# Diagonal blocks of A of chunks 0 and 1 in one set of columns, one transpose for three, one scale for all input weights, and a new order: a delta-rule attention with a feed-forward layer behind it

## The chip, the cores and the metric

One core of a Trainium2 chip runs the whole program. Times are device microseconds (us) of one execution. In the profile PE is the matmul engine TensorE (PEld its weight loads), DVE is VectorE, ACT is ScalarE, POOL is GpSimd and SP is SyncE, whose queue issues all DMAs of this kernel.

## What is computed

The reference walks 768 tokens for 4 batches of 8 heads with a head dimension of 48, and then runs a feed-forward layer on the result:

```python
for t in range(S):
    kt, vt, bt = (k_n[:, :, t], v[:, :, t], beta[:, :, t, None])
    y[:, :, t] = np.einsum('bhd,bhde->bhe', q[:, :, t], state)
    v_old = np.einsum('bhde,bhd->bhe', state, kt)
    state = state + bt[:, :, :, None] * np.einsum('bhd,bhe->bhde', kt, vt - v_old)
...
h = x @ w_in                       # x: 3072 tokens x 384, w_in: 384 x 2048
sp = np.maximum(h, 0.0) + np.log1p(np.exp(-np.abs(h)))
g = h * erf(sp)
return (g @ w_out).astype(np.float32)
```

`k_n` is k over its norm. The weights arrive as 64-bit floats.

## The kernel before

**Chunks.** The tokens are cut into 12 chunks of 64. Within a chunk the recurrence is a triangular system: a Gram matrix of the keys of each head (`gram_mm`), scaled by beta and the norms into A (`gram_a`, or `gram_ac` and `gram_am`), and the inverse of the unit triangular matrix that A makes. The two heads of a pair lie on the two halves of the 128 partitions, and 16 pairs (`BP`) stand side by side. The inverse is found for 32 by 32 diagonal blocks by substitution (`solve_row`), and `merges` joins two such blocks with small matmuls (`merge_e`, `merge_z`). Then `merge_m`, `chain_u`, `chain_s` and `chain_y` carry the state from chunk to chunk and give y.

**Chunks 0 and 1** are done first and apart. A of both lies in `A01`, `[128, 2, 16, 64]`, in a part of the room of `w_out` that is not loaded yet. `block_t` turns its diagonal blocks into `gb`. The first call turns columns 32 to 63 for all partitions, which is right for the lower 32 rows of each head; the second and third turn columns 0 to 31 for the upper 32 rows of each head. 15 steps of `row16` then solve 16 by 16 blocks on VectorE, `small_t` and `back_t` turn the result back, and `small_e`, `small_z` and `merges` put the pieces together. Chunks 2 to 11 go in five pairs: A is written to DRAM, read back as blocks (`to_dram`, `to_blocks`), solved in 31 rows mostly on GpSimd, and sent back the same way (`put_blocks`, `from_blocks2`).

**Feed-forward.** Each chunk gives 256 tokens, group g. `ffn1` multiplies by 16 blocks of `w_in`, `e_sp`, `e_erf`, `e_mul`, `e_split` and `e_rest` make the gate and split it into two f16 halves, and `ffn2` multiplies by 16 blocks of `w_out`. Group 0 uses the weights as f32. From group 1 on, weights and activations are pairs of f16 numbers under a scale that is a power of two: `x_max`, `x_all` (a matmul that spreads a maximum over all partitions) and `x_scale` find it for the activations; `w_max`, `w_all` and `w_scale` for the weights; `w_hi` and `w_lo` write the two halves over the f32 block before. Before that each piece of the weights is loaded as 64-bit numbers (`w_load`) and made f32 by `w_mask`, `w_sign`, `w_bits`, while `w_mx` takes its maximum. The input weights are in two parts: "in", the first 4 blocks in two pieces, and "in2", the other 12 in eight pieces, each part with a maximum and a scale of its own.

**Order.** All calls are first put on a list. `ORDER` is a permutation of its indices, written out by hand: the calls are made in that order, and each engine, SP with its DMAs too, runs its instructions in the order in which they were made. `ENG` names, for some places, another engine than the default. `put_v` for instance multiplies v by the key norms on GpSimd (G) unless `ENG` says VectorE (V). `fill` is a matmul of zeros whose result nobody reads; there are `WF` = 233 of them, placed by `ORDER` like everything else.

Of the kernel before, what the change touches and what calls it, by code (L numbers as in the profile page):

```python
# [15 lines left out]
P = 128  # L16
# [17 lines left out]
ORDER = (0, 1, 2, 3, 4, 46, 15, 9, 12, 8, 19, 22, 24, 27, 28, 23, 29, 30, 31, 16, 32, 33, 34, 25, 20, 2232, 2233, 2234, 2235, 2236, 2237, 2238, 2239, 2240,  # L34
# [131 lines left out]
XR = 3  # L166
YR = 3
CM = (0, 1)
WF = 233
GF = 1  # L170
TK = {}

# [6 lines left out]
def delta_ffn_kernel(ctx, tc, kT, qT, ktok, vtok, btok, w_in, w_out, cst, out):  # L179
# [313 lines left out]
    def block_t(k):  # L493
        if 0 not in gb_t:
            gb_t[0] = wide("gb", 0)
# [719 lines left out]
```

## Time and profile before

| | |
|---|---|
| median of 3 runs | 618.2 us (616.4 to 619.39) |
| the profiled execution | 621.86 us, its span 620.1 us |
| TensorE busy | 577.6 us, 93% of the span, 11,125 matmuls |
| VectorE busy | 452.4 us, 73% |
| ScalarE busy | 421.1 us, 68%, of it 157.8 us in 123 table loads |
| GpSimd busy | 285.8 us, 46% |
| fills | 233, 47.7 us of the time of TensorE |
| mean granted TensorE clock | 0.965 of full speed |

The span runs from the first to the last instruction. The 1.8 us between it and the execution's time lie around the program. A busy share is a mean over stages that differ; the tables by stage below say which engine has no idle time where.

### The profile page before, as it was taken

To read this page: it belongs to the slowest core of one execution; us is meant where nothing else is said; L and a number is where in the kernel's file an instruction comes from. 1 tells how busy PE (TensorE), PEld (TensorE's weight loads), DVE (VectorE), ACT (ScalarE), POOL (GpSimd) and SP (SyncE) were. 2 spreads that over 40 slices of the span, in tenths; PEclk is the share of its full clock that TensorE was granted. 3 is DMA by queue.
4 is the path that set the end of the run, shared out by engine and by line. 5 is a ranking of instruction groups with operands and counts; after the bars stand their busy time and mean duration, and the time that the engine had idled before them with its cause. 6 is when DMAs were issued, how large, how long until landed. Compare 5 with 4: busy or idle time off the path is not lost.

```text
span 620.1 us, 25280 instructions
## 1 busy us (share of the span) xinstructions
PE 577.6 (93%) x11125; PEld 425.6 (69%) x11125; DVE 452.4 (73%) x1006; ACT 421.1 (68%) x602; POOL 285.8 (46%) x475
## 2 busy tenths in 40 slices
PE   7943698999999999999999999999999999999996
PEld 5622466677667787777777787767777787777673
DVE  5996588897998788887887976679675776354321
ACT  2326447667767687847976888477769688589862
POOL 7031124577489874668738670438853021001310
PEclk8976599999999999999999999999999999999999
DMA  9984549737913258655460618450542320101011
GB/s 273 300 243 118 131 135 218 189 90 176 178 23 97 56 139 203 156 136 135 95 132 4 183 29 205 98 84 17 140 96 64 68 61 2 27 1 27 1 26 26
DMA packets 79502, 67.89 MB, mean 109 GB/s; under 512 B 57696, under 2 KB 67040, under 8 KB 79136
## 3 DMA queue, kind: packets, MB, share of 16 engines
q1 hardware_dynamic: 79392, 66.28, 43.7%
q8 instruction: 87, 1.43, 1.0%
q14 instruction: 23, 0.19, 0.1%
HBM read 47.38 MB, written 17.83 MB: 105 GB/s over the span
## 4 chain that ended last, share of the span: by engine, by line
PE 70%; DVE 13%; issue 5%; DMA 5%; POOL 3%; ACT 2%; SPq 1%; ACTq 0%; POOLq 0%; DVEq 0%
PE ph L921 26%; PE pr L980 9%; PE pr L982 9%; PE pr L981 9%; PE pc L680 3%; PE pc L706 2%; DMA qp<-qT 2%; PE pg L407 2%; PE pc L694 2%; PE pc L710 2%; PE pm L643 1%; PE pe L611 1%; POOL tmp L525 1%; PE pz L626 1%; POOL xb L527 1%
## 5 line engine op out<-in xcount | busy, mean ns | idle before, releaser
L921 PE MATMUL ph<-xh,w_in 128*128 128x256 f16 x1056 | 188.2, 273 | 0.3 <-DVE L L955 0.3
L921 PEld LDWEIGHTS <-w_in 128*128 128x128 f16 x1584 | 151.6, 98 | 25.4 <-issue 0.5
L253 ACT ACT_TABLE_LOAD x123 | 157.8, 1283 | 2.9 <-PEq L1208 0.7
L921 PE MATMUL ph<-xl,w_in 128*128 128x256 f16 x528 | 143.9, 273 | 0.0
L980 PE MATMUL pr<-w_out,H 128*128 128x384 f16 x352 | 115.1, 327 | 0.0
L981 PE MATMUL pr<-w_out,H 128*128 128x384 f16 x352 | 114.8, 326 | 0.0
L982 PE MATMUL pr<-w_out,H 128*128 128x384 f16 x352 | 114.8, 326 | 0.0
L210 POOL TENSOR_TENSOR H<-L,H 128x512 f16<-128x512 f32 x42 | 49.9, 1199 | 127.7 <-ACT H L215 97.4
L955 DVE SCALAR_TENSOR_TENSOR L<-ph,L 128x512 f32<-128x512 f32 x88 | 59.8, 685 | 55.2 <-ACT L L948 52.0
L943 ACT ACTIVATE L<-ph,xct 128x512 f32<-128x512 f32 x88 | 58.8, 687 | 49.4 <-PE ph L921 39.6
L525 POOL TENSOR_TENSOR tmp<-gb,xb 128x175 f32<-128x175 f32 (+15 forms) x120 | 66.0, 550 | 49.5 <-DVE xb L527 23.4
L527 POOL TENSOR_TENSOR xb<-xb,tmp 128x175 f32<-128x175 f32 (+15 forms) x120 | 70.7, 589 | 9.4
L948 ACT ACTIVATE L<-L 128x512 f32<-128x512 f32 x96 | 58.5, 626 | 0.8
L210 POOL TENSOR_TENSOR z<-v,nm 64x192 f32<-64x192 f32 x60 | 32.2, 537 | 48.1 <-DMA v<-vtok 33.1
L982 PEld LDWEIGHTS <-H 128*128 128x128 f16 x352 | 34.4, 98 | 22.8
L263 PE MATMUL pr<-zero 128*128 128x384 f16 x233 | 47.7, 354 | 1.2 <-DVE zero L259 1.2
L980 PEld LDWEIGHTS <-H 128*128 128x128 f16 x352 | 34.4, 98 | 20.1
L981 PEld LDWEIGHTS <-H 128*128 128x128 f16 x352 | 34.5, 98 | 17.8
L215 ACT CAST H<-L 128x512 f16<-128x512 f32 x54 | 32.3, 613 | 13.6 <-DVE L L955 11.6
L699 DVE TENSOR_TENSOR z<-pc,z 48x192 f32<-48x192 f32 x86 | 30.4, 354 | 15.0 <-PE pc L694 10.3
L210 DVE TENSOR_TENSOR H<-L,H 128x512 f16<-128x512 f32 x46 | 38.5, 845 | 1.6 <-ACT H L215 1.2
L686 DVE TENSOR_TENSOR z<-pc,ga 64x192 f32<-64x192 f32 x94 | 33.4, 355 | 6.1 <-PE pc L680 3.9
(205 smaller groups left out, 946.4 us busy)
## 6 DMA issues: line engine op xcount, KB each, us to landing
raw_out<-w_out SPq DMA_DIRECT2D x12, 512.0 KB, 6.4
d<-pp SPq DMA_DIRECT2D x10, 512.0 KB, 4.7
d<-A SPq DMA_DIRECT2D x20, 256.0 KB, 3.2
qp<-d SPq DMA_DIRECT2D x20, 256.0 KB, 4.8
k<-ktok SPq DMA_DIRECT2D x12, 384.0 KB, 4.3
kpg<-kT SPq DMA_DIRECT2D x24, 192.0 KB, 5.3
v<-vtok SPq DMA_DIRECT2D x48, 96.0 KB, 3.0
qp<-qT SPq DMA_DIRECT2D x24, 192.0 KB, 4.2
```

What stands on the lines that cost most here:

```text
L210: {"V": ve, "G": ge}[pick(d)].tensor_tensor(*a, **kw)
L253: se.add_instruction(mybir.InstLoadActFuncSet(name=nc.get_next_instruction_name(), act_func_set_id=i, ins=[], outs=[]))
L263: te.matmul(pr[1][:, :DM], zero[:, :P], zero[:, :DM], start=new, stop=new)
L525: eng.tensor_tensor(tv, g.unsqueeze(1).broadcast_to([P, ncol, nr]), Xv[:, :, s:s + 1].broadcast_to([P, ncol, nr]), op=ALU.mult)
L527: eng.tensor_tensor(Xv[:, :, s + 1:], Xv[:, :, s + 1:], tv, op=ALU.add)
L921: te.matmul(ph, w[:, i, kt * P:kt * P + P], G[x][:, :, ksl], start=(m == 0), stop=(m == 8))
L943: se.activation(unit(g, u), G["ph", u], AF.Softplus, bias=0.0, scale=G["ct"][:, part(EU * u):part(EU * u) + 1] if g >= GF else 1.0)
L948: se.activation(Lu, Lu, AF.Erf, bias=0.0, scale=1.0)
L955: ve.scalar_tensor_tensor(Lu, fg[g]["ph", u], HSC, Lu, op0=ALU.mult, op1=ALU.mult)
L980: te.matmul(G["po"][a], gh[:, o, asl], wout_h[:, i, :], start=(i == 0), stop=False)
L981: te.matmul(G["po"][a], gh[:, o, asl], wout_l[:, i, :], start=False, stop=False)
L982: te.matmul(G["po"][a], gl[:, o, asl], wout_h[:, i, :], start=False, stop=(i == NFF - 1))
```

## The change

`gram_mm` of chunks 0 and 1 makes each 64 by 64 product of the keys in two matmuls of 32 stationary columns. The first writes the upper 32 rows with all 64 columns. The second writes the lower 32 rows with columns 32 to 63, twice side by side. So columns 0 to 31 of `A01` hold the diagonal block of every group of 32 partitions, and one `block_t` turns them all; `small_e` reads them there. "in" and "in2" become one part of ten pieces with one maximum and one scale (`NA` = 16, `RI`), and the columns of scales shrink from two to one. `WF` goes from 233 to 281. `ORDER` (2,465 entries, now 2,508) and `ENG` are replaced as a whole; the 48 added fills, less two `block_t` and the three calls `w_max`, `w_all`, `w_scale` of the second part, are the 43 more.

```diff
-RI = {"in": "EH", "in2": "EHLHLHLH"}
-NA = 4
+RI = {"in": "EHEHLHLHLH"}
+NA = 16
...
-WF = 233
+WF = 281
...
                 for hb in range(2):
-                    rhs = kf if name == "pg" else qp[c % 2][hb]
-                    te.matmul(st[c][name, i][r(1 - hb), o, :], kf[rd(hb), oo, :], rhs[rd(hb), oo, :], start=True, stop=True)
+                    if name == "pq":
+                        te.matmul(st[c][name, i][r(1 - hb), o, :], kf[rd(hb), oo, :], qp[c % 2][hb][rd(hb), oo, :], start=True, stop=True)
+                        continue
+                    b0, k = C - hb * C, kf[rd(hb), oo, :]
+                    te.matmul(st[c][name, i][b0:b0 + 32, o, :], k[:, :32], k, start=True, stop=True)
+                    te.matmul(st[c][name, i][b0 + 32:b0 + 64, o, :].rearrange("p (w x) -> p w x", w=2), k[:, 32:], k[:, 32:].unsqueeze(1).broadcast_to([D, 2, 32]), start=True, stop=True)
...
     def block_t(k):
-        if 0 not in gb_t:
-            gb_t[0] = wide("gb", 0)
-        q, f = (slice(0, P), 1) if k == 0 else (slice((k - 1) * C, (k - 1) * C + 32), 0)
-        ve.transpose(gb_t[0][q].rearrange("p s t -> p t s"), A01[q].rearrange("p c a x -> p (c a) x")[:, :, f * 32:f * 32 + 32].rearrange("p m t -> p t m"))
+        gb_t[0] = wide("gb", 0)
+        ve.transpose(gb_t[0].rearrange("p s t -> p t s"), A01.rearrange("p c a x -> p (c a) x")[:, :, :32].rearrange("p m t -> p t m"))
...
-                te.matmul(pe[q0:q0 + 32, o, :], A01[q0:q0 + 32, c, o, f * 32:f * 32 + 32], small(c)[q0:q0 + 32, o, :], start=True, stop=True)
+                te.matmul(pe[q0:q0 + 32, o, :], A01[q0:q0 + 32, c, o, :32], small(c)[q0:q0 + 32, o, :], start=True, stop=True)
...
-    for k in range(3):
-        on(block_t, k)
+    on(block_t, 0)
```

What the two orders call on TensorE at the start, read off the lists (a gram call is one half of the 16 pairs of one chunk):

| before | after |
|---|---|
| 19 fills; the four grams of the keys | 10 fills; both grams of chunk 0; 46 fills; both of chunk 1 |
| 42 fills; the four grams of q | 62 fills; the four grams of q |
| 17 fills; `w_all` of "in"; 22 fills; `small_e` | 11 fills; `small_e` |

The first loads were k of chunks 0 and 1, then the transposed keys of chunks 1 and 0 (`load_kf`). Now they are, in this order: the transposed keys of chunk 0, k of chunks 3, 0 and 1, one v, q of chunk 1, k of chunk 2, one v, beta, one piece of `w_in`, and the transposed keys of chunk 1. The one `w_scale` of the input weights stands behind `ffn1` of blocks 0 and 1 of group 0.

## Rows read from the trace of the kernel before

**Rows 1.** Busy time by stage: length, busy us (instructions) of each engine, PEclk, DMA, GB/s.
```profile
0.00:10.00 10.00, 6.10 (x21) 2.81 (x21) 3.97 (x4) 2.97 (x3) 9.41 (x19) 0.99 0.84 206
10.00:50.00 40.00, 29.16 (x584) 21.69 (x585) 37.04 (x87) 9.32 (x13) 10.25 (x22) 0.83 0.87 265
50.00:80.00 30.00, 15.38 (x627) 11.19 (x630) 18.04 (x37) 16.33 (x33) 3.28 (x5) 0.54 0.49 128
...
160.00:180.00 20.00, 18.57 (x546) 13.02 (x536) 19.29 (x38) 11.41 (x21) 13.67 (x22) 1.00 0.56 97
180.00:190.00 10.00, 9.85 (x196) 6.72 (x195) 8.99 (x25) 9.30 (x16) 8.98 (x15) 1.00 0.35 92
190.00:605.00 415.00, 413.91 (x7693) 310.50 (x7692) 294.20 (x651) 314.24 (x421) 197.41 (x325) 1.00 0.36 83
```

**Rows 2.** Busy time of the first 180 us and of the rest, the same columns.
```profile
0.00:180.00 180.00, 144.83 (x3185) 103.15 (x3186) 146.78 (x328) 94.73 (x161) 78.09 (x136) 0.89 0.68 178
```

**Rows 3.** Timeline of PE: start, us, instruction, operands, count, idle before it and its releaser.
```profile
1.19 5.77 PE L263 MATMUL pr<-zero 128*128 128x384 f16 x19 [1.19 <-DVE zero L259]
...
10.08 5.27 PE L403 MATMUL pg<-kpg 48*64 48x64 f32 x93 [0.90 <-DMA kpg<-kT]
...
16.88 7.00 PE L263 MATMUL pr<-zero 128*128 128x384 f16 x42
...
64.41 0.29 PE L572 MATMUL py<-xm,T 32*16 32x16 f32 x11 [4.32 <-issue]
...
109.86 1.45 PE L975 MATMUL pr<-w_out,L 128*128 128x384 f32 x4
```

**Rows 4.** The spread matmul of group 2: count, ns min/median/max, first and last start.
```profile
L757 PE MATMUL sp<-ident,xm x2: 272/274/275, 188.5 to 188.7; 128*128 128x128 f32 x2
```

**Rows 5.** Timeline of DVE, columns as for PE.
```profile
18.31 4.05 DVE L497 STREAM_TRANSPOSE gb<-w_out 128x1024 f32<-128x1024 f32 x2
...
22.72 1.92 DVE L497 STREAM_TRANSPOSE gb<-w_out 32x1024 f32<-32x1024 f32 x1
...
39.23 0.15 DVE L810 TENSOR_REDUCE m_in<-mx_in 128x1 f32<-128x2 f32 x1
...
45.66 3.23 DVE L210 TENSOR_TENSOR pp<-pp,mask 128x512 f32<-128x512 f32 x1
```

**Rows 6.** Groups of DVE and POOL: operation, tiles, count, busy us, mean ns, idle before.
```profile
L210 DVE TENSOR_TENSOR H<-L,H 128x512 f16<-128x512 f32 x46 | 38.5, 845 | 1.6 <-ACT H L215 1.2
L686 DVE TENSOR_TENSOR z<-pc,ga 64x192 f32<-64x192 f32 x94 | 33.4, 355 | 6.1 <-PE pc L680 3.9
...
L527 DVE TENSOR_TENSOR xb<-xb,tmp 128x231 f32<-128x231 f32 (+14 forms) x35 | 12.8, 366 | 1.2
...
L217 DVE COPY T<-pe 32x256 f32<-32x256 f32 x26 | 11.0, 422 | 4.2 <-ACT T L215 2.5 <-PE pe L611 1.2
...
L210 DVE TENSOR_TENSOR A<-A,gn 128x512 f32<-128x512 f32 x2 | 1.4, 684 | 0.0
...
L210 POOL TENSOR_TENSOR z<-v,nm 64x192 f32<-64x192 f32 x60 | 32.2, 537 | 48.1 <-DMA v<-vtok 33.1 <-PE pc L694 4.9 <-DVE z L686 3.3
```

**Rows 7.** The chain that ended last, its longer pieces: start, us, engine, tile, line, count.
```profile
191.51 1.04 PE pm L643 x64
...
195.33 0.82 PE pc L680 x64
...
199.70 1.09 PE ph L921 x9
```

**Rows 8.** Groups of PE from 93.15 to 94.26 us, columns as in the groups above.
```profile
L407 PE MATMUL pg<-kpg 48*64 48x64 f32 x32 | 1.1, 221 | 0.0
L407 PE MATMUL pq<-qpg,kpg 48*64 48x64 f32 x32 | 1.1, 221 | 0.0
```

**Rows 9.** Timeline of POOL, columns as for PE.
```profile
45.86 2.48 POOL L210 TENSOR_TENSOR pp<-pp,mask 128x512 f32<-128x512 f32 x2
```

**Rows 10.** DMA issues: count, KB each, us from issue to landing.
```profile
d<-xb SPq DMA_DIRECT2D x10, 256.0 KB, 3.7
...
xm<-d SPq DMA_DIRECT2D x40, 64.0 KB, 2.8
```

More of the change, by code (lines that the diff above doesn't have):

```diff
@@ L32 @@
 HALF = BP // 2
-ORDER = (0, 1, 2, 3, 4, 46, 15, 9, 12, 8, 19, 22, 24, 27, 28, 23, 29, 30, 31, 16, 32, 33, 34, 25, 20, 2232, 2233, 2234, 2235, 2236, 2237, 2238, 2239, 2240,
[94 rows of a table removed]
-ENG = {48: 'G', 49: 'G', 50: 'G', 51: 'G', 53: 'G', 55: 'G', 56: 'G', 58: 'G', 61: 'G', 68: 'A', 70: 'V', 78: 'V', 79: 'A', 86: 'A', 90: 'V', 92: 'V', 99:
[21 rows of a table removed]
+ORDER = (0, 1, 3, 2, 12, 44, 20, 2227, 2228, 2229, 2230, 2231, 2232, 2233, 2234, 2235, 2236, 35, 14, 4, 13, 508, 19, 22, 23, 5, 24, 512, 27, 513, 28, 29, 227,
[96 rows of a table added]
+ENG = {45: 'G', 47: 'G', 49: 'G', 50: 'G', 56: 'G', 59: 'G', 64: 'A', 65: 'V', 66: 'A', 68: 'V', 77: 'A', 84: 'A', 87: 'V', 90: 'V', 94: 'V', 97: 'V', 98:
[20 rows of a table added]
 UM = 32
 DZ = 64
-RI = {"in": "EH", "in2": "EHLHLHLH"}
-NA = 4
+RI = {"in": "EHEHLHLHLH"}
+NA = 16
 LPE = {"in": (), "out": ()}
@@ L733, in delta_ffn_kernel @@
     wn = {"in": "in", "in2": "in", "out": "out"}
-    c_in = con.tile([P, 2], F32, name="c_in")
-    m2in = con.tile([P, 2], F32, name="m2in")
+    c_in = con.tile([P, len(RI)], F32, name="c_in")
+    m2in = con.tile([P, len(RI)], F32, name="m2in")
     c_out = con.tile([P, 1], F32, name="c_out")
@@ L738, in delta_ffn_kernel @@
     for nm in tags:
-        wt[nm] = {k: con.tile([P, n], F32, name=f"{k}_{nm}") for k, n in (("mx", len(cut[nm])), ("m1", 1), ("m2", 1), ("s0", 1), ("sc", 2 if nm == "out" else 1))}
+        wt[nm] = {k: con.tile([P, n], F32, name=f"{k}_{nm}") for k, n in (("mx", len(cut[nm])), ("m1", 1), ("m2", 1), ("s0", 1), ("sc", len(RI) if nm == "out" else 1))}
     for i, nm in enumerate(RI):
@@ L876, in x_max @@
         for k in ("m1", "m2", "sx", "ct", "co"):
-            G[k] = sm.tile([P, 2 if k == "ct" else 1], F32, tag="x" + k, bufs=5, name=f"x{k}{g}")
+            G[k] = sm.tile([P, len(RI) if k == "ct" else 1], F32, tag="x" + k, bufs=5, name=f"x{k}{g}")
         ve.tensor_reduce(G["m1"], mg[g], axis=AX.X, op=ALU.max)
```

231 rows, old and new, of tables (ENG, ORDER) are left out of this document.

## The prediction, as it was put on record

> **What bounds the kernel now.** I read the table by stage first. From 190 to 605 us TensorE is busy for 413.91 of 415 us at the full clock, so nothing that the other engines save there shortens the run [rows 1]. From 160 to 180 us VectorE is busy for 19.29 of 20 us, 97%, while TensorE still has gaps; from 180 to 190 it is the reverse, 8.99 against 9.85 of 10 [rows 1]. So VectorE sets the pace up to about 188 us and TensorE from there to the end. The mark between them is the spread matmul of group 2 at 188.5 us [rows 4]. The run ends earlier by as much as VectorE reaches this mark earlier, and by the TensorE work that lies ahead of the mark in the new order and was behind it in the old one.
>
> In its first 180 us VectorE is busy for 146.78 us [rows 2]; the 33 us of gaps are 6.0 us before the first norms, 12.0 us between 50 and 80 us, and small ones [rows 1]. TensorE is idle for 35 us of the same time [rows 2], so fills have room there. Between 50 and 80 us its granted clock is 0.54, nearly all at the lower of its two levels, 1.2 of 2.4 GHz [rows 1]. The timeline shows it standing for up to 4.32 us in a row for no engine's sake ("issue") between small matmuls, and VectorE then waits for what it evicts [rows 3].
>
> **The transposes and the scale.** The three calls of `block_t` took 4.05 us for two and 1.92 us for one, the narrow ones no less than the wide one [rows 5]. One stays: 4.0 us less on VectorE. Joining the scales removes one `w_max` and `w_scale`: nine small instructions, the first of them with 0.15 us at 39.23 us [rows 5], about 1.5 us of VectorE. TensorE's wait for that first maximum goes too, which I count at nothing: the solve on VectorE covers it, and without that cover it would show as a later `small_e`. All of `w_hi` now has to wait for the last of ten pieces; by the list, though, the one `w_scale` has fewer VectorE instructions ahead of it than the old second one had, so I count no loss.
>
> **The new order, up to the mark.** I went through both lists and counted which calls go to VectorE ahead of the spread of group 2. Besides the terms above, these leave: 5 `put_v`, two instructions each of the size that takes 0.36 us (-3.6); 2 `merge_e2`, a `merge_z2` and a `back_x`, seven copies of 0.42 us (-2.9); 2 evictions of 128x512 at about 0.69 us (-1.4); 2 `chain_y2` at 0.36 us (-0.7); a norm sum and a `w_lo` at about 0.7 us each (-1.4). These come: 4 rows of the block solve, two instructions of 0.37 us each (+2.9); 3 `gram_am` at 0.68 us (+2.1); 2 `e_rest` at 0.85 us (+1.7); 2 `chain_u2` with two of 0.36 us (+1.4); a `merge_m2` and an `e_mul` at about 0.69 us (+1.4); two more `w_sign` (+0.4) [rows 6]. Leaving 10.0, coming 9.9: the moves balance, and the net of VectorE is that of the two edits, 5.5 us and a little, say 5.6. At 97% busy that is 5.8 us of time.
>
> For this VectorE time the new list has more TensorE work done at the mark: two `ffn1` blocks (1.09 us each), one `merge_m` (1.04), two `chain_u` (0.82 together) and one f32 block of `ffn2` (1.45) [rows 3, 7]. That is 5.5 us that TensorE, which has no gaps afterwards, needn't do any more.
>
> **The grams and the 46 fills at the start.** The key grams go from 128 instructions to 256. At the lower clock the old ones started every 57 ns (93 in 5.27 us) [rows 3]; two ran at a time. The new halves use four different parts of the array in turn. The nearest rows are grams of later chunks, where 64 instructions in four parts took 1.1 us, 17 ns each, at the full clock [rows 8]. So four at a time cost no more than two did before. The Trainium skill (TensorE: Matmul & The Clock Gate, The mechanism) says that a weight load overlaps matmuls in flight only where its row group differs; the two halves of a block share theirs. By that rule two would run at a time, and the 128 instructions behind the fills would take 4 us instead of 2.2; the rows of later chunks, whose pairs share their rows too, don't agree.
>
> The wait is elsewhere: the grams of chunk 1 now stand behind 46 fills. Chunk 0's keys are loaded first, so I let its 128 instructions end at about 10 us, a little before the old grams were half through. Fills cost 304 ns at the lower clock (19 in 5.77 us) and 167 ns at the full one (42 in 7.00 us) [rows 3]; some two thirds at the full clock make about 9 us, and the last grams end at about 21 us. The old ones ended at 16.9 us, where the next fills begin [rows 3]. The 3.3 MB queued up to chunk 1's keys need until 13 to 15 us at 206 and then 265 GB/s [rows 1], which the fills hide. The norms have a little more in front of them on VectorE than before and are hidden too. I take +4 us for VectorE's wait before `gram_a`. The bounds: full clock from the start, grams done at 18 us, +1; lower clock throughout, 7.3 us of grams, 14 us of fills and 7.3 us of grams from 5 us on, +16.
>
> The other 62 fills wait beside the solve and 43 more come behind `ffn1` of block 16, all ahead of the mark. 48 more in all are 8.0 us at 167 ns, against 35 us of idle time there: nothing, and 8 us if that cover were gone.
>
> **The gap between 50 and 80 us.** Ahead of `small_t` VectorE has some 11 us less to do: the 4.0 and 1.5 us above, and evictions, masks and `w_bits` that now come later. So the merges of chunk 0 start earlier, with that work behind them to fill the waits. No row shows how much it fills: between nothing and all 12.0 us. I take 4 us, the size of the longest stand of TensorE there [rows 3].
>
> **Sum.** -5.8 - 5.5 + 4 - 4 = -11.3 us. The profiled execution took 621.86 us, 1.8 us around its span, and would take 610.6 us. It lies 3.7 us above the median of 618.2 us, to which I apply the same difference: 607 us. This measurement can tell 0.5%, 3.1 us, from no change: 615.1 to 621.3 us is the same.
>
> **The rivals.**
> *The gap closes:* with warm matmuls and work behind each wait, all 12.0 us go: 8 us more, 599 us. For it: half the clock and idle engines there. Against it: "issue" waits have no releaser in the trace, and the small matmuls are as many as before.
> *GpSimd's share comes back:* a mask product of 128x512 took 3.23 us on VectorE at 45.66 us, against 0.68 us for that size elsewhere, while GpSimd ran two like it [rows 5, 6, 9]. If each of the ten `put_v` instructions that left VectorE holds one up for the 0.54 us it takes on GpSimd [rows 6], 5.4 us return: 612 us. The Trainium skill (SBUF — State Buffer, Who interferes with whom) has it that a VectorE instruction with two SBUF inputs contends with a GpSimd instruction that reads SBUF, and that the later one is blocked; the 3.23 us row agrees.
> *A cold start:* if TensorE gets the lower clock through all 46 fills, the front costs +16 instead of +4: 619 us, no change. Against it: the old fills ran at 167 ns right after 6.9 us of grams.
> *Slower, a late solve:* behind the mark TensorE covers nothing. Of pair 5 the list now has about 11 us of TensorE work between the last solve row and `merge_e`, where it had some 30. The two DMAs between take 3.7 and 2.8 us [rows 10], and two transposes some 1.4: 8 us. What GpSimd is late beyond 3 us is lost one for one; from 17 us late the run is slower than 621 us, say 623. Against it: GpSimd is busy for under half of that stretch [rows 1].
> *The change doesn't do what it says,* two halves at a time only: 128 x 31 instead of 17 ns, 2 us, inside the range below.
>
> **Chances.** Forecast (600 to 613 us) 0.46, the gap closes 0.14, GpSimd's share 0.12, a cold start 0.14, a late solve 0.14. Faster: 0.46, 0.14 and 0.08 of GpSimd's, which ends astride the bound, 0.68. Same: 0.04 and 0.14, 0.18. Slower: 0.14. The range goes from 597 us, the closed gap with a fast front, to 620 us, the cold start; it leaves out the late solve and a little below. The likeliest case's own range is 600 to 613.
>
> **What would show it.** Right: one transpose of about 2 us; the last gram of chunk 1 at 19 to 23 us; `small_t` and the first f32 `ffn1` some 10 us earlier; the spread of group 2 before 186 us; TensorE at 99% behind it. Wrong: the granted clock at 0.5 up to 20 us; VectorE's gap at 50 to 80 us only moved; TensorE idle behind the mark on `merge_e`; or VectorE still at 97% long after group 2, because work pushed back falls due there.

## The result, and the profile after

| | before | after | ratio, 95% interval |
|---|---|---|---|
| first comparison | 617.6 us (4 runs, 616.4 to 619.39) | 611.05 us (4 runs, 610.08 to 612.62) | 0.9864 [0.9832, 0.9896] |
| again, beside the last experiments | 619.56 us (19 runs) | 613.69 us (8 runs) | 0.9909 [0.9876, 0.9942] |

The change is faster. By the two ratios it gains 0.9 to 1.4% of 618 us, 5.6 to 8.4 us, where the prediction had 11.3. The profiled execution after took 610.08 us, its span 608.3. Set against the span of before, 620.1, that is 11.8 us, but before's profiled execution lay 3.7 us above its median and this one lies 1.0 us below its own. The profiled executions of e9 and e11 below were the longest of their kernels, so their spans are not used.

The table by stage of the kernel after, columns as in [rows 1]:

```profile
0.00:10.00 10.00, 8.79 (x159) 5.37 (x160) 2.40 (x4) 3.59 (x4) 6.24 (x13) 1.00 0.77 237
10.00:50.00 40.00, 27.56 (x741) 19.32 (x738) 32.79 (x81) 14.73 (x24) 16.24 (x34) 0.85 0.94 291
50.00:80.00 30.00, 22.95 (x742) 16.41 (x741) 22.91 (x49) 15.49 (x32) 5.30 (x7) 0.68 0.41 121
160.00:180.00 20.00, 18.60 (x574) 14.01 (x560) 17.34 (x40) 13.79 (x27) 13.19 (x26) 1.00 0.60 145
190.00:595.00 405.00, 403.24 (x7432) 303.15 (x7430) 280.16 (x652) 306.40 (x416) 176.83 (x291) 1.00 0.37 83
```

VectorE's idle time from 50 to 80 us went from 12.0 to 7.1 us. From 10 to 50 us it went from 3.0 to 7.2 us. Up to 80 us it is idle no less than before; the gap has moved to the front of that stretch. TensorE is again all but full behind 190 us.

The mark, the spread matmul of group 2, columns as in [rows 4]:

```profile
L760 PE MATMUL sp<-ident,xm x2: 272/274/275, 182.4 to 182.5; 128*128 128x128 f32 x2
```

It comes 6.2 us earlier than in [rows 4]. The stretch from the mark to the end, of before and then of after, in the columns of the stage table:

```profile
188.54:620.10 431.56, 424.37 (x7753) 316.68 (x7752) 297.84 (x661) 318.15 (x428) 200.08 (x327) 1.00 0.35 81
```

```profile
182.38:608.30 425.92, 418.50 (x7603) 312.86 (x7602) 289.21 (x670) 313.92 (x427) 183.37 (x300) 1.00 0.35 80
```

Behind the mark there are 150 matmuls and 5.9 us of busy TensorE less. Its idle time there is 7.2 and 7.4 us, the same. So the 11.8 us between the spans split at the mark into 6.2 ahead and 5.6 behind.

That split hangs on where the mark is put. The spread matmul one group earlier, that of group 1, starts at 143.3 us before and at 130.6 after. The stretches ahead of it and behind it, of before and then of after:

```profile
0.00:143.30 143.30, 109.85 (x2423) 78.33 (x2423) 114.01 (x263) 69.63 (x119) 54.74 (x99) 0.86 0.69 190
143.30:620.10 476.80, 467.73 (x8704) 347.23 (x8702) 338.40 (x743) 351.47 (x484) 231.03 (x377) 1.00 0.37 85
```

```profile
0.00:130.64 130.64, 109.16 (x2636) 77.51 (x2637) 100.96 (x229) 68.95 (x115) 62.59 (x112) 0.88 0.71 205
130.64:608.30 477.66, 468.72 (x8664) 348.62 (x8662) 332.08 (x773) 354.70 (x500) 208.39 (x344) 1.00 0.38 86
```

Behind this spread both kernels take the same time, 476.8 and 477.7 us, with TensorE idle for 9 of them. So the whole gain, 12.7 us less 0.9, lies ahead of group 1. TensorE does no less work in the whole span (577.6 and 577.9 us); it is idle for 12 us less, all of it ahead of this spread. VectorE has 13.1 us less to do there, and its idle time is the same, 29.3 and 29.7 us.

VectorE's timeline at the front, columns as in [rows 5]:

```profile
16.79 1.29 DVE L433 TENSOR_TENSOR w_out<-pg,gn 128x512 f32<-128x512 f32 x2
...
19.90 1.98 DVE L500 STREAM_TRANSPOSE gb<-w_out 128x1024 f32<-128x1024 f32 x1
...
25.99 0.69 DVE L807 TENSOR_REDUCE mx_in<-raw_in 128x1 f32<-128x512 f32 x1 [2.13 <-DMA raw_in<-w_in]
...
35.55 1.06 DVE L554 STREAM_TRANSPOSE T<-xb 128x512 f32<-128x512 f32 x1
```

One transpose of 1.98 us stands where 5.97 us stood [rows 5]. New is a wait of 2.13 us for the load of a piece of `w_in` in the middle of the solve. `small_t` (L554) starts at 35.55 us; before, it started at 44.81.

TensorE's timeline, columns as in [rows 3]:

```profile
5.30 0.22 PE L407 MATMUL pg<-kpg 48*32 48x64 f32 x1
5.31 0.22 PE L408 MATMUL pg<-kpg 48*32 48x64 f32 x1
5.32 0.22 PE L407 MATMUL pg<-kpg 48*32 48x64 f32 x1
5.33 0.22 PE L408 MATMUL pg<-kpg 48*32 48x64 f32 x1
5.36 0.22 PE L407 MATMUL pg<-kpg 48*32 48x64 f32 x1
...
6.63 7.65 PE L264 MATMUL pr<-zero 128*128 128x384 f16 x46
14.86 0.24 PE L407 MATMUL pg<-kpg 48*32 48x64 f32 x1 [0.58 <-DMA kpg<-kT]
...
36.67 2.20 PE L566 MATMUL pf<-T,w_out 32*32 32x16 f32 x221 [2.17 <-DVE T L554]
43.89 0.66 PE L566 MATMUL pf<-T,w_out 32*32 32x16 f32 x34 [5.02 <-issue]
...
49.19 0.47 PE L575 MATMUL py<-xm,T 32*16 32x16 f32 x36 [3.62 <-issue]
...
54.48 0.50 PE L575 MATMUL py<-xm,T 32*16 32x16 f32 x37 [3.51 <-issue]
...
77.07 2.76 PE L919 MATMUL ph<-y,w_in 128*128 128x256 f32 x12
```

The first f32 `ffn1` is at 77.07 us, 12.0 us earlier than before. The "issue" waits in the bursts of small matmuls (`small_e`, L566, and `small_z`, L575) add up to 12.2 us. Between the first and the second wait the timeline counts 127 matmuls, between the second and the third 127 and a fill. The page's rows on DMA queues that carry instructions, of the kernel after (packets, MB, share of 16 engines), offer a cause:

```profile
q8 instruction: 88, 1.44, 1.0%
q14 instruction: 23, 0.19, 0.1%
```

The span executes 25,600 instructions; 1.63 MB over these are 64 bytes each, and one packet of 1.44 MB / 88 = 16.4 KB holds 256 of them, or 128 matmuls with their weight loads. 88 such packets are 22,528 instructions; TensorE has 22,598 matmuls and weight loads. The same view, with the data's queue (q1), between 36 and 56 us:

```profile
q1 hardware_dynamic: 1770, 4.15, 81.3%
q8 instruction: 3, 0.05, 1.0%
```

Three packets of instructions, three waits. The view of a narrow window tells when a packet starts. These are the windows 41.3 to 41.4, 46.5 to 46.6 and 52.0 to 52.1 us:

```profile
q8 instruction: 1, 0.02, 73.5%
```

```profile
q8 instruction: 1, 0.02, 54.9%
```

```profile
q8 instruction: 1, 0.02, 68.4%
```

The share gives a packet's time: 73.5% of 16 engines over 0.1 us are 1.18 us. So the first packet runs from 41.3 to 42.5 us, inside the wait from 38.9 to 43.9; the second to 47.4, inside 45.6 to 49.2; the third to 53.2, inside 51.0 to 54.5. TensorE goes on 1.3 to 1.8 us behind the end of each. The same holds for all 40 issue waits of 1.3 us or more in these bursts, in the 14 executions with a trace: one packet each, which takes 0.9 to 1.6 us, and TensorE goes on 1.2 to 1.9 us behind its end. So these waits are the arrival of TensorE's next instructions. A wait is long where its packet starts late, up to 4.4 us after TensorE has stopped.

The Trainium skill (Trainium Architecture — The Big Picture, The software stack) says that an instruction has 64 bytes, which agrees, and that the streams are brought to the engines when the program is loaded; these rows have them come in during the run.

### The profile page after: what moved, and what is told of

It reads as the page before. It is cut to its first block, busy times and chain, and to the rows that moved or that the text cites. A ratio compares the mean times of both kernels' runs of the same rounds, so it can differ in the third digit from the quotient of the medians.

```text
span 608.3 us, 25600 instructions
## 1 busy us (share of the span) xinstructions
PE 577.9 (95%) x11299; PEld 426.1 (70%) x11299; DVE 433.0 (71%) x1001; ACT 423.7 (70%) x614; POOL 271.0 (45%) x455
## 3 DMA queue, kind: packets, MB, share of 16 engines
q1 hardware_dynamic: 79392, 66.28, 43.9%
q8 instruction: 88, 1.44, 1.0%
## 4 chain that ended last, share of the span: by engine, by line
PE 72%; DVE 12%; DMA 6%; issue 4%; POOL 3%; SPq 1%; ACT 1%; POOLq 0%; ACTq 0%
PE ph L924 25%; PE pr L983 9%; PE pr L985 8%; PE pr L984 8%; PE pc L683 3%; DMA raw_in<-w_in 3%; PE pc L709 2%; PE pr L264 2%; PE pr L978 2%; PE pc L697 2%; PE pg L412 2%; PE ph L919 2%; PE pc L713 2%; PE pm L646 1%; DMA raw_out<-w_out 1%
## 5 line engine op out<-in xcount | busy, mean ns | idle before, releaser
L211 POOL TENSOR_TENSOR H<-L,H 128x512 f16<-128x512 f32 x39 | 45.5, 1172 | 145.3 <-DVE H L218 75.9
L528 POOL TENSOR_TENSOR tmp<-gb,xb 128x31 f32<-128x31 f32 (+15 forms) x112 | 60.3, 538 | 55.1 <-DVE xb L530 32.5
L530 POOL TENSOR_TENSOR xb<-xb,tmp 128x31 f32<-128x31 f32 (+15 forms) x112 | 67.7, 605 | 8.8
L211 POOL TENSOR_TENSOR z<-v,nm 64x192 f32<-64x192 f32 x60 | 33.4, 557 | 58.4 <-DMA v<-vtok 29.3
L264 PE MATMUL pr<-zero 128*128 128x384 f16 x281 | 54.3, 343 | 1.2 <-DVE zero L260 1.2
L264 PEld LDWEIGHTS <-zero 128*128 128x128 f16 x281 | 26.7, 101 | 20.5 <-issue 3.4
L702 DVE TENSOR_TENSOR z<-pc,z 48x192 f32<-48x192 f32 x86 | 30.4, 353 | 14.3 <-PE pc L697 10.8
L211 DVE TENSOR_TENSOR H<-L,H 128x512 f16<-128x512 f32 x49 | 34.6, 710 | 4.1 <-ACT H L216 3.8
```

Of the source, the lines that this page charges most:

```text
L211: {"V": ve, "G": ge}[pick(d)].tensor_tensor(*a, **kw)
L264: te.matmul(pr[1][:, :DM], zero[:, :P], zero[:, :DM], start=new, stop=new)
L528: eng.tensor_tensor(tv, g.unsqueeze(1).broadcast_to([P, ncol, nr]), Xv[:, :, s:s + 1].broadcast_to([P, ncol, nr]), op=ALU.mult)
L530: eng.tensor_tensor(Xv[:, :, s + 1:], Xv[:, :, s + 1:], tv, op=ALU.add)
```

## The experiments

Theory at the start: the terms of the prediction add up, two transposes and one scale on VectorE's path, TensorE's work ahead of the mark, and the front. Rival: the order makes the gain and the new forms are hidden, by the wait for a load and by the issue waits, which are the arrival of instructions behind data.

The expected times go by the first comparison. Beside the experiments the kernel before took 619.6 to 619.8 us, 2.0 to 2.2 more, so 2 us come off a measured time before it is held against its forecast; the ratios need no such step.

**e1: the old form of the diagonal blocks in the new order.**

```diff
-                    te.matmul(st[c][name, i][b0:b0 + 32, o, :], k[:, :32], k, start=True, stop=True)
...
+                    rhs = kf if name == "pg" else qp[c % 2][hb]
+                    te.matmul(st[c][name, i][r(1 - hb), o, :], kf[rd(hb), oo, :], rhs[rd(hb), oo, :], start=True, stop=True)
...
-    on(block_t, 0)
+    for k in range(3):
+        on(block_t, k)
```

> The changed kernel with the old form of the diagonal blocks (128 grams, three transposes of 2.0 us) in the new order. Sum theory (the two transposes stand on the path): small_t starts 4.0 us later than 35.55 us, and the time is some 4 us over the changed kernel's, 615 us. Rival (the front waits for a load of w_in and the matmul bursts behind it wait for something else, so the transposes are covered): small_t at most 2 us later, the time within 1 us of 611 us.

Measured: 612.6 us, 0.9894 [0.9865, 0.9923], about the rival's forecast. `small_t` starts at 37.57 us, 2.0 us later for 4.0 us more work; the wait of 2.13 us for the load of `w_in` is gone. The issue waits are 4.25, 2.87 and 4.06 us, together 1.0 less. The first f32 `ffn1` is at 76.8 us, no later than in the kernel after, and the mark at 185.2. The intervals of e1 and of both comparisons of the kernel after overlap: the new form is worth less than can be told here.

**e2: the new order alone,** e1 with the two parts of the input weights as well.

```diff
-RI = {"in": "EHEHLHLHLH"}
-NA = 16
+RI = {"in": "EH", "in2": "EHLHLHLH"}
+NA = 4
```

> The new order with both old forms: old diagonal blocks and two scales for the input weights. Sum theory (forms 5.5 us, order the rest): 616 to 617 us, about the kernel before. Rival (the order makes the whole gain): 611 to 612 us. What lies between says how much of the gain is the order's.

Measured: 611.55 us, 0.9877 [0.9847, 0.9906], so 7.6 us by the order alone. The mark is at 185.7 us, the first f32 `ffn1` at 79.1. The rival's forecast came, or a little less, and the ratio is as low as the changed kernel's. The second scale can't be seen in the time.

**e3: the new blocks in the old order,** the kernel before with the new `gram_mm`, `block_t` and `small_e`.

```diff
-    for k in range(3):
-        on(block_t, k)
+    on(block_t, 0)
```

> The kernel before with only the new form of the diagonal blocks (256 smaller grams, one transpose), old order and two scales. Sum theory: small_t 4 us ahead of 44.81 us and the time 4 us under the kernel before, 613.5 us. Rival (in the old order, waits behind the transposes swallow it): within 1 us of 617.6 us.

Measured: 616.48 us, 0.9943 [0.9925, 0.9961], 3.5 us faster than before. VectorE's `small_t` and TensorE's first f32 `ffn1`:

```profile
42.28 0.99 DVE L553 STREAM_TRANSPOSE T<-xb 128x512 f32<-128x512 f32 x1
```

```profile
84.20 4.15 PE L918 MATMUL ph<-y,w_in 128*128 128x256 f32 x18
```

These are 2.5 and 4.9 us earlier than in the kernel before, and the mark is 4.5 us earlier, at 184.0. Here the term of 4.0 us holds within its interval (2.4 to 4.6 us), though `small_t` comes only 2.5 us earlier: the 256 grams, at the lower clock in this order and with a 1.8 us issue wait among them, end at 18.7 us instead of 16.9, and the transpose starts 1.7 us later. The two parts of the change don't seem to add: 3.5 us alone, 7.6 us alone, 5.6 to 8.4 us together. The intervals are too wide to be sure of it.

**e4: chunk 1's bursts behind chunk 0's chain.** `small_e` and `small_z` of chunk 1 and their evictions go behind `chain_s` and `chain_y`.

```diff
-        T = at.tile([P, 512], F32, tag="T", name="T16")
+        T = at.tile([P, 512], F32, tag="A2", name="T16")
...
+        return ps1.tile([P, 512], F32, tag="ph", name=name) if c else pbank(name)
```

> The changed kernel with the two bursts of chunk 1 (256 small matmuls, L566 and L575) issued behind the first chain step of chunk 0, and T16 in the buffer of A2. Theory (TensorE's issue waits of 5.0, 3.6 and 3.5 us in the bursts of chunks 0 and 1 stand on the path, about one per 128 matmuls, whatever they work on): two of the three leave the way to the first merge, the first merge_e starts at 47 to 50 us instead of 56.3, the first f32 ffn1 near 70 us instead of 77, the time 605 to 607 us. Rival (VectorE's weight work, which ends with w_max at 79 us, or the same waits at another place hold the start of the projection): first f32 ffn1 within 2 us of 77 us, the time within 1.5 us of 611 us.

Measured: 616.95 us, 0.9964 [0.9941, 0.9987], 3 to 6 us slower than the kernel after by its two ratios. TensorE's timeline:

```profile
43.36 0.95 PE L578 MATMUL py<-xm,T 32*16 32x16 f32 x92 [5.05 <-ACT xm L216]
...
58.88 0.85 PE L632 MATMUL pz<-xm,T 32*32 32x32 f32 x46 [2.11 <-issue]
...
64.22 0.53 PE L686 MATMUL pr<-z,xm 128*32 128x48 f32 x13 [2.04 <-issue]
```

The two large waits left the way to the merges, which begin at 52.9 us instead of 56.3. But issue waits came up in `merge_z` and `chain_u` and took that back, `small_z` waited 5.05 us for ScalarE, and the chunk 1 work then stood ahead of `ffn1`, whose first f32 matmul slipped to 81.4 us. The theory's first half held, its time didn't; the rival's time didn't come either.

**e5: the new order up to the mark, the old one behind it.**

```diff
-ORDER = (new order)
+ORDER = (new order up to the spread of group 2, then the old order without what is issued)
```

> The changed kernel up to the spread matmul of group 2 in the new order, everything behind it in the old order with the old engines. From that matmul to the end of the span the kernel before took 431.6 us and the changed one 425.9. Theory (the 5.7 us are TensorE's work that the new order has done ahead of the mark): 425 to 427 us behind the mark, time within 1.5 us of the changed kernel's 611 us. Rival (the new tail itself is better, by where the late solves and the differences run): 430 to 432 us behind the mark, 616 to 617 us.

Measured: 624.02 us, 1.0073 [1.0042, 1.0103]: both missed. Behind the mark, and the wait that stood out there (columns: engine, line, releaser, us, times, longest):

```profile
182.26:620.10 437.84, 421.75 (x7603) 313.80 (x7601) 292.84 (x657) 317.10 (x425) 191.50 (x319) 0.99 0.33 77
```

```profile
DVE T L604 <- DMA xm<-d: 7.8, 1, 7.8
```

The mark is early (182.3 us) and the same 150 matmuls are done ahead of it, but TensorE is idle for 16.1 us behind it, 9 us more than with the new tail, 6.9 of it between 220 and 240 us, where VectorE waits for a solve to come back. The granted clock falls to 0.79 there, and the same matmuls take 3.3 us more busy time behind the mark. TensorE's work ahead of the mark is a gain only with a tail whose solves keep up with it. Which moves of the new tail do that wasn't tried.

**e6: no wait for the load in the solve.** The maximum and the sign of piece 9 of `w_in` go behind `back_t`.

```diff
-ORDER = (..., row 2, w_mx in 9, row 3, row 4, w_sign in 9, ..., back_t 1, ...)
+ORDER = (..., row 2, row 3, row 4, ..., back_t 1, w_mx in 9, w_sign in 9, ...)
```

> The changed kernel with the maximum and the sign word of part 9 of w_in behind the second back_t, so that VectorE doesn't wait for that load in the solve (2.13 us at 23.9 us). Theory (the issue waits behind small_t take up what the front gains): small_t at 31.5 to 32 us instead of 35.55, the issue waits in the bursts together longer by most of it, the spread of group 2 within 1.5 us of 182.4 us, time 609 to 611 us. Rival (the path runs from the solve to the end one to one): the spread near 179 us and 607 to 608 us.

Measured: 612.42 us, 0.9901 [0.9867, 0.9935]; the mark at 184.1. VectorE's `small_t`, and TensorE behind it:

```profile
33.69 1.06 DVE L554 STREAM_TRANSPOSE T<-xb 128x512 f32<-128x512 f32 x1
```

```profile
37.71 1.27 PE L566 MATMUL pf<-T,w_out 32*32 32x16 f32 x128 [1.37 <-issue]
46.37 0.66 PE L566 MATMUL pf<-T,w_out 32*32 32x16 f32 x34 [7.39 <-issue]
```

`small_t` is 1.9 us earlier and the issue waits in `small_e` are 3.7 us longer. What the front gains is waited for behind it. `small_t` was expected at 31.5 to 32 us; it lost the rest ahead of the solve, where this execution's first `gram_a` is at 18.59 us. The time fits the theory, the mark misses its 1.5 us narrowly.

**e7: two more transfers,** copies that nobody reads, queued at 30 us.

```diff
+    def copy_more(i):
+        d = dr.tile([P, 2048], I32, tag="more", bufs=2, name=f"more{i}")
+        sp.dma_start(d, w_in.bitcast(I32)[:, 2048 * i:2048 * i + 2048])
```

> The changed kernel with two copies of 1 MB from DRAM to DRAM, read by nothing, queued behind the load of part 2 of w_in. Theory (TensorE's issue waits are the arrival of its next instructions, 16 KB for 128 matmuls with their weight loads, behind data transfers on the same DMA engines): the wait at small_e grows from 5.0 us to 8 us or more, at the same place in the burst, 35 matmuls before its end. Rival (the wait belongs to the matmuls themselves, or to data that isn't shown): 4.5 to 5.5 us as before.

Measured: 619.69 us in one run. **e8: two loads later,** pieces 2 and 6 of `w_in`, 1.5 MB, and what reads them, from 28 us to 46 us.

```diff
-ORDER = (..., w_load in 0, w_load in 6, w_load in 2, ..., put_p 1, ...)
+ORDER = (..., w_load in 0, ..., put_p 1, w_load in 2, w_load in 6, ...)
```

> The changed kernel with the loads of parts 2 and 6 of w_in (1.5 MB), and what reads them, behind the put of chunk 1's P. Theory (issue waits are fetches behind transfers): the wait of 5.0 us at small_e falls to 1 to 3 us, those at small_z stay or grow as the loads come there; the first f32 ffn1 1 to 4 us ahead of 77 us, time 608 to 611 us. Rival (the waits don't depend on the transfers): 4.5 to 5.5 us as before, and the later weights cost 1 to 3 us, 612 to 614 us.

Measured: 613.29 us, 0.9901 [0.9863, 0.994]. The two are read together. TensorE's waits of e7 and then of e8:

```profile
43.69 0.66 PE L570 MATMUL pf<-T,w_out 32*32 32x16 f32 x34 [5.08 <-issue]
...
51.46 0.47 PE L579 MATMUL py<-xm,T 32*16 32x16 f32 x36 [6.28 <-issue]
...
59.83 0.49 PE L579 MATMUL py<-xm,T 32*16 32x16 f32 x37 [6.25 <-issue]
```

```profile
41.55 0.72 PE L566 MATMUL pf<-T,w_out 32*32 32x16 f32 x35 [1.77 <-issue]
...
46.54 0.47 PE L575 MATMUL py<-xm,T 32*16 32x16 f32 x36 [2.62 <-issue]
...
53.20 0.50 PE L575 MATMUL py<-xm,T 32*16 32x16 f32 x37 [4.88 <-issue]
```

The stages from 36 us, of after, e7 and e8; the column before the last is the DMA engines' busy share:

```profile
36.00:46.00 10.00, 3.88 (x348) 3.58 (x349) 9.80 (x14) 9.16 (x15) 6.16 (x10) 0.62 0.83 226
46.00:56.00 10.00, 3.30 (x169) 2.12 (x168) 4.52 (x9) 4.97 (x10) 1.00 (x2) 0.50 0.81 195
```

```profile
36.00:46.00 10.00, 3.54 (x348) 3.33 (x349) 9.80 (x14) 7.79 (x12) 2.33 (x3) 0.65 1.03 351
46.00:56.00 10.00, 1.97 (x128) 1.38 (x127) 3.70 (x7) 5.89 (x11) 3.44 (x7) 0.50 1.04 207
```

```profile
36.00:46.00 10.00, 4.76 (x348) 4.46 (x349) 9.80 (x14) 7.94 (x14) 6.38 (x10) 0.54 0.45 109
46.00:56.00 10.00, 4.58 (x227) 3.06 (x229) 5.59 (x11) 2.43 (x5) 0.00 (x0) 0.50 1.01 305
```

With the copies the second and third wait grew from 3.6 and 3.5 us to 6.3 each, at the same matmuls; with the loads away from the first burst its wait fell from 5.0 to 1.8 us (and 0.7 before `small_z`), and the third, now beside them, grew to 4.9. The waits follow the transfers and not the matmuls. What the transfers move is the start of the packet: in e7 the second and third start 3.5 us after TensorE has stopped, in the kernel after 1.0 and 1.1; in e8 the first starts 1.1 us before it stops, and no data moves during that wait. The 0.7 us before `small_z` have no packet and stay unexplained. The first wait of e7 didn't grow, against the expectation: its packet starts at 41.1 us, in the kernel after at 41.3. No row shows when it was asked for. e7's mark came 9.1 us late, e8's at 185.0 although its first `ffn1` was 1.1 us early; e8's time lies between the theory's and the rival's.

**e9: six more transposes** in `block_t`, the same one written over itself.

```diff
+        for _ in range(7):
             ve.transpose(gb_t[0].rearrange("p s t -> p t s"), ...)
```

> The changed kernel with the one transpose written seven times over itself: 11.9 us more of VectorE ahead of the solve. Theory (what is late in front of small_t is partly taken up by the load wait of 2.13 us and by issue waits that shrink once the transfers have drained): small_t near 45.5 us, the issue waits in the bursts together 5 to 9 us instead of 12.2, the spread of group 2 4 to 8 us behind 182.4, the time 615 to 619 us. Rival (one to one): the spread at 192 us or later, 621 us or more.

Measured: 619.34 us, 0.9994 [0.9964, 1.0024]; beside it the kernel after took 613.69. `small_t` is at 47.17 us, 11.6 later, the issue waits are 7.6 us together, and the run is 5.7 us longer: about half a microsecond for one ahead of `small_t`, as the theory had it. The mark of its one trace, at 195.9 us, is the rival's, but that execution took 8.5 us more than the median.

**e10: without the 46 fills** at the start.

```diff
-ORDER = (..., gram_mm 0 1, 46 fills, gram_mm 1 1, ...)
+ORDER = (..., gram_mm 0 1, gram_mm 1 1, ...)
```

> The changed kernel without the 46 fills between the grams of chunks 0 and 1. Sum theory as predicted (gram_a waits 4 us behind the fills): the first gram_a some 4 us earlier, 607 us. Rival 1 (TensorE would wait for the keys of chunk 1 until 14.9 us anyway): first gram_a within 0.3 us of 16.79 us, the time within 1.5 us of the changed kernel's. Rival 2 (the fills buy the clock): a granted clock of 0.5 from 15 us on, the 128 grams 2 us longer, 613 us.

Measured: 612.96 us, 0.9899 [0.986, 0.9937], the mark at 181.3. The first gram of chunk 1 on TensorE, the first `gram_a` on VectorE, and the stage from 10 us:

```profile
15.09 0.31 PE L405 MATMUL pg<-kpg 48*32 48x64 f32 x1 [7.71 <-DMA kpg<-kT]
```

```profile
17.94 1.29 DVE L431 TENSOR_TENSOR w_out<-pg,gn 128x512 f32<-128x512 f32 x2 [1.15 <-PE pg L406]
```

```profile
10.00:20.00 10.00, 4.45 (x130) 3.85 (x131) 8.12 (x29) 0.84 (x1) 4.11 (x16) 0.50 0.97 313
```

TensorE waits 7.71 us for the keys of chunk 1 where the fills were, at the lower of its levels then, and `gram_a` is 1.2 us later than in the kernel after. By itself that shows little: in eight executions with the fills it starts between 16.65 and 18.59 us. The sum theory falls. The keys hold these grams up, as rival 1 has it. The clock of rival 2 is there as well: from the last wait for keys to the last gram it takes 3.6 us instead of 2.0. Neither reaches the time.

**e11: three loads of `w_out` later,** issued behind those of 54 us instead of at 11 to 13 us.

```diff
-ORDER = (..., w_load out 4, ..., w_load out 3, ..., w_load out 0, ..., w_load out 8, ...)
+ORDER = (..., w_load out 8, w_load out 4, w_load out 3, w_load out 0, ...)
```

> The changed kernel with the three loads of w_out that it issues at 11 to 13.5 us (1.5 MB) and their first readers put behind the chain of chunk 0. Theory (the front and the bursts wait for the transfers that are queued ahead): the wait of 2.13 us for part 9 of w_in goes, the transfers of w_in have drained some 4 us sooner, the first issue wait falls to 1 to 3 us, the first f32 ffn1 at 71 to 74 us, the spread of group 2 at 177 to 181 us, 606 to 609 us. Rival (what is loaded later stands in the way later): the issue waits of the merges and of the chain grow by what the bursts gain, the spread within 1.5 us of 182.4 us, 610 to 613 us.

Measured: 613.14 us, 0.9893 [0.9843, 0.9943]. The wait of 2.13 us is gone and `small_t` is at 33.03 us, but the bursts then have issue waits of 3.5, 2.2, 3.3 and 3.5 us, together as much as in the kernel after. No gain, as the rival had it, though the waits stayed in the bursts. The first f32 `ffn1`, expected at 71 to 74 us, is at 78.6, and the mark at 191.5, in the longest execution of this kernel.

**e12: the kernel after, again.**

> The changed kernel as it is, beside the three others on their chip: 0.983 to 0.990 of the kernel before; the spread of group 2 at 182 to 184 us and 425 to 427 us from there to the end.

Measured: 0.9909, as in the table at the top. The mark came at 185.2 us, and 429.1 us passed behind it; all three lie outside what was expected. The mark is 2.8 us and the stretch behind it 3.1 us more than in the first execution: the granted clock was 0.66 from 176 to 181 us, and TensorE had 3.3 us of gaps between 190 and 300 us. So 3 us between two single executions mean nothing here, around the mark or behind it. The spread of group 1 is steadier: 130.4 us here, 130.6 in the first execution.

## Why the prediction was right, and where it wasn't

The direction and the range were right. The gain is half to three quarters of the forecast.

**TensorE's work ahead of the mark, -5.5.** The count was right: 150 matmuls and 5.9 us. e1, e2, e4, e6, e7, e8 and e10 keep it, with 424.7 to 426.7 us from the mark to the end against 431.6. e3, with the old order, needs 431.1. But it is no gain of its own. The step that failed is the place of the mark. From the spread of group 1 to that of group 2 TensorE is idle for only 1.9 us before and 1.5 after, so work put in there makes that stretch longer, 51.7 us instead of 45.2. With the spread of group 1 as the mark this term is nothing: TensorE is busy behind it for 467.7 us before and 468.7 after. What the prediction left out as well is that the tail has to be made for the new order (e5).

**The transposes, -4.0, and the scale, -1.5, "at 97% busy".** The durations were right, one transpose of 1.98 us. The step that failed is to let them count in full in the new order. In the old order the transposes are worth 3.5 us (e3); in the new one they and the scale are worth less than the 3 us or so that two such intervals can tell (e1, e2). At the spread of group 1 single executions have them at 2.5 us: 130.6 us, and 133.1 in e2. In the new order VectorE waits for a load in the solve, which the transposes merely fill, and for TensorE's instructions behind `small_t`. The busy share of 160 to 180 us, from which I took the 97%, says nothing of the front.

**The gap between 50 and 80 us, -4.** Wrong as put: it moved to 40 to 60 us, as the text named for a failure. The issue waits aren't matmuls that could be warmer, nor work that could be nearer, but instructions that arrive beside 4 MB of transfers. The shorter the front, the longer they tend to be. From `small_t` to the first f32 `ffn1` it takes 44.2 us with `small_t` at 33.7 us (e6), 41.5 at 35.6 (after), 39.2 at 37.6 (e1) and 36.8 at 47.2 (e9). Single executions stray from that by some 2 us: 38.7 at 35.7 in e5, 41.9 at 37.2 in e2.

**The 46 fills, +4.** Wrong: the first `gram_a` is at 16.79 us, and the last gram of chunk 1 ends at 17.6, not at 19 to 23. The 46 ran at the full level, 166 ns each, and end at 14.3 us; the keys come at 14.9, or 15.1 in e10. I had the keys between 13 and 15 us and the grams of chunk 0 until 10 us. They end at 6.7, since four of the new halves start within 56 ns. My two thirds at the full level give 9.8 us for the 46 fills, not 9. The rule of the Trainium skill (TensorE: Matmul & The Clock Gate, The mechanism), that a weight load overlaps matmuls in flight only where its row group differs, by which two would run at a time, doesn't hold in this trace either: 14 ns each, for halves that share their rows.

**The sum.** -5.8 + 4 - 4 for the mark came to -5.8, and single executions show -6.2 and -3.4. That is right by accident: the +4 isn't there, the two edits give little of the -5.8 in the new order, and the gap behind the -4 only moved. What moved the mark is the order ahead of it, which I had counted as balanced. In e2, without the new forms, the mark is 2.8 us earlier than before, and `small_t` 7.6 us earlier, by work that now stands behind it; half of such a gain is lost behind `small_t` (e9). Up to the spread of group 2 VectorE is busy for 10.7 us less, not 5.6: four of the norms' instructions took 4.2 us before and 0.7 after, five mask products 6.1 and 3.7, which a count from the lists cannot see. Up to that of group 1 it is busy for 13.1 us less, and for 11.2 less in e2 with both old forms, and the spread comes 12.7 and 10.2 us earlier. That VectorE's work sets this spread is read from the sums of single executions; which moves do it wasn't tried.

**The rivals.** The gap didn't close, the clock was full through the fills, and four halves ran at a time. The late solve isn't there: TensorE is idle for 1.8 of 405 us behind 190 us. With the old tail it is (e5). GpSimd's share had no run of its own, and the traces have the opposite: up to 182 us VectorE's five mask products of 128x512 took 1.21 us on the mean before and 0.74 after.

## What to carry to other kernels

A saving on a busy engine counts only as far as the next wait that isn't that engine's: run the edits alone and together, since here 3.5 and 7.6 us alone gave 5.6 to 8.4 together. Split the span at the point where one engine becomes full, and look for the first such point: at the spread of group 2 half of the gain looked like work done early, at that of group 1 all of it lies in front. Compare the busy time behind it, which is steady: from the spread of group 2 on 418.5 to 419.7 us in ten executions of the new order (e9 had 420.8), while the span of one kernel moved by 6 us from one execution to another. An order that does work early needs the rest of the order to match it.

## What the hardware showed beyond that

TensorE's instructions come in packets of 16.4 KB during the run, in the same microseconds as the data. In bursts of matmuls that start every 10 ns (221 in 2.20 us) 128 last 1.3 us, and the wait for the next was up to 7.4 us beside DMA engines at their full share (e6) and 1.8 us in e8, where no data moved during the wait. Two copies of 1 MB made two of three such waits 2.7 us longer each. A packet itself took 0.9 to 1.6 us, in light traffic and in heavy; what changed was when it started, 1.1 us before TensorE stopped up to 4.4 us after. That the fetch queues with the data is what these runs speak for; when a packet was asked for isn't in the rows.
